# Decode attention with a mixer MLP on one core: x fetched as 16 rows, p turned half by half, exponents read from PSUM, maxima taken bank by bank

## The chip, the core and the metric

The kernel runs on one core of a Trainium2 chip. The metric is the device time of one launch in microseconds (us); the figure for a kernel is the median of its runs. The profile is one more execution, recorded by the hardware profiler.

## What is computed

For two batch rows `x` (2 x 1 x 1024, all in fp32) two branches are mixed by a gate:

```python
g = _sigmoid((x * gate_w).sum(-1, keepdims=True))
a = _A_ref(x, A_k_cache, A_v_cache, A_wq, A_wo)
b = _B_ref(x, B_w1, B_w2, B_w3, B_w4)
return g * a + (1 - g) * b
```

Branch A is attention for one new token against a long cache: 32 query heads share 4 key/value heads, the cache has 32768 positions of 128 numbers for each of the 8 pairs (batch row, key/value head). Branch B is a layer norm and a gelu MLP of 1024 -> 3584 -> 1024 (with one position the shifted part of the mixer adds nothing, so `w1` and `w2` are not used).

```python
q = (x @ wq) -> 32 heads of 128
scores = einsum("bhqd,bhkd->bhqk", q, k) * (Dh ** -0.5)
p = softmax(scores);  o = einsum("bhqk,bhkd->bhqd", p, v)
a = o @ wo
h2 = gelu(layernorm(x1) @ w3) @ w4          # x1 = x here;  b = x1 + h2
```

Every weight and the whole cache is read once: 331.37 MB.

## The kernel before, in words

**One stream through two buffers.** All large operands pass through two SBUF buffers, `buf_a` and `buf_b`, each 128 partitions of up to 64 KB. SyncE (SP) issues the loads in one fixed order (L554 to L567), alternating: `wq` to a, `w3` to b, `wq`, `w3`, then for every pair two loads of keys (`kt`, to a) and two of values (`vt`, to b), with `w4` and `wo` woven in. The first two loads go out at once. Every later one waits on the semaphore `go`, which VectorE (DVE) raises in `free()` (L284) when TensorE (PE) has finished with a buffer. So a buffer is loaded again only after its matmuls are over, and the DMA queue has work as long as one buffer is always issued before the other one's load ends. The last load (`w4`, second part) comes in five pieces (L571).

**Rounds.** PE runs 20 rounds (`rounds`, L136). In each it multiplies the load in `buf_a` (`sets(0, ...)`, into the two PSUM banks `ps_a`) and then that in `buf_b` (`sets(1, ...)`, into `ps_b`). The small stationary operands, `wt_a` and `wt_b`, hold x, the queries, or p; semaphores `ready[0]` and `ready[1]` say that they are filled. A pair takes two rounds: in the first its second scores meet the first half of its values, in the second the next pair's first scores meet the second half of its values.

**x.** ScalarE (ACT) fetches `xg` (x and the gate vector, laid out as 128 partitions of 24 numbers) with one DMA into `x2` (L195): each of the 64 rows of 48 numbers is read twice, once for the lower and once for the upper half of the partitions, and the access pattern has that factor of 2 outermost. DVE waits for it (`edge`, L319), shuffles it into `xs` (L322), and the gate, mean, variance and `wt_a` for the first `wq` load follow from it in a chain through DVE, PE and ACT (L326 to L359). No load's matmul can start before `wt_a` is there.

**From scores to p.** DVE takes the maximum over both banks (`scores`, L418) and copies the scores to SBUF (`keep`, L421); for a pair's second scores the maximum goes through a PE transpose, a reduction and a PE broadcast to become `bias` (L482 to L490). ACT then takes four exponents, one for each bank of the first and second scores (L217 to L220). Each is taken twice (`spread_rows`, L208), which writes p into all eight 128-column blocks of `p_dup` with every block twice. PE multiplies the eight blocks by the permutation `perm` (L161) into both banks of `tr`, and DVE copies `tr` into `wt_b` with two copies over 64 partitions (`turned`, L473). As each exponent fills all of `p_dup` and each turn all of `tr`, exponent, turn and copy of one bank are over before those of the next begin. A pair does this twice in its first round and twice in its second.

**Queries.** GpSimd (POOL) writes the next pair's queries to `wt_a` (L247) when `dp` says that the scores have been copied out of `ps_a`.

Of the kernel before, what the change touches and what calls it, by code (L numbers as in the profile page):

```python
# [24 lines left out]
E = 2  # L25
# [14 lines left out]
def kernel(  # L40
# [32 lines left out]
    ident, ones, perm = (sbuf(n, P) for n in ("ident", "ones", "perm"))  # L73
    r32 = sbuf("r32", C)
# [4 lines left out]
    mask_g, mask_r = sbuf("mask_g", 1), sbuf("mask_r", 1)  # L79
    x2 = sbuf("x2", 2 * KD * 3)  # L80
    xs = sbuf("xs", KD * 3)
# [8 lines left out]
    h_fin = sbuf("h_fin", FIN * C)  # L90
    mx, m1, bias = sbuf("mx", 2), sbuf("m1", 1), sbuf("bias", 1)
    m8, mb = sbuf("m8", REP, 1), sbuf("mb", P, 1)
# [11 lines left out]
    with tc.tile_critical(sync_engine=POOL, no_gpsimd_drain=True):  # L104
# [16 lines left out]

        def sets(x, which, event=False):
            last = None
# [6 lines left out]
            if event:  # L130
                last.then_inc(pd, 1)

# [3 lines left out]
        def rounds():  # L136
            with t.Fori(0, ROUNDS) as i:
                with t.If(i > 0):
                    sets(1, range(5, 8), True)
                    with odd(i):  # L140
                        take(t, dvp)
                        mm(sm[:, LP:LP + REP], ones, lsel).then_inc(pd, 1)
                        take(t, dvp)
                        for e in range(E):
                            last = mm(sm[:, OP + e * REP:OP + (e + 1) * REP],
                                      pv_t[:, e * P:(e + 1) * P], sel_all)
                        last.then_inc(pd, 1)
                take(t, landed[0], 16)
                take(t, ready[0])
                sets(0, range(8), True)  # L150
                with t.If(i < ROUNDS - 1):
                    with odd(i):
# [13 lines left out]
                take(t, piece, 16)  # L166
                sets(1, range(3, 5), True)
            done = 0
# [16 lines left out]
        with t.Fori(0, 2) as phase:  # L185
            with t.If(phase > 0):
                rounds()
            with t.Else():
                take(t, dvp)
# [5 lines left out]
        s.dma_start(x2, bass.AP(xg.tensor, xg.offset, [[0, 2], [2 * KD * 3, H], [1, 2 * KD * 3]])  # L195
                    ).then_inc(edge, 16)
        take(s, da)
# [5 lines left out]

        def spread_rows(src, bank, func, n, **kw):

            for d in range(2):
                more = kw if d == 0 else {k: x for k, x in kw.items() if k != "accum_out"}
                last = s.activation(at(p_dup, d * H, (512, 2), (P, 4), (1, H)),  # L208
                                    at(src, bank * 512, (1, 2), (P, 4), (2, H)), func, **more)
            last.then_inc(acp, n)  # L210

        for src in (qs, hs):
            take(s, da)
            spread_rows(src, 0, AF.Copy, 2)
# [9 lines left out]
        g_.memset(ident, 0.0)  # L224
        g_.drain()
        g_.affine_select(out=ident, in_=ident, compare_op=ALU.not_equal, fill=1.0, base=0,
                         pattern=[[-1, P]], channel_multiplier=1).then_inc(pc, 1)
        for tt in (sel, wt[0], wt[1], h_fin, buf[1][:, E * F * 2:], p_dup, lsel, pv_t):
            g_.memset(tt, 0.0)
# [70 lines left out]
        v.memset(mb, 0.0)  # L300
        v.wait_ge(pc, 1)
        v.tensor_reduce(r32, ident.rearrange("p (j c) -> p c j", j=G), axis=AX.X, op=ALU.add)
        for i in range(2):
            v.tensor_reduce(parity[:, i:i + 1], at(ident, i * C, (2 * C, 2), (1, C)), axis=AX.XY, op=ALU.add)
        for tau in range(2):
            for u in range(2):
                v.tensor_copy(at(perm, tau * H + u * C, (REP, G), (1, REP)),
                              at(ident, 16 * u + REP * tau, (C, G), (1, REP)))
        wait_order()
# [8 lines left out]

        v.wait_ge(edge, 16)  # L319
        for W in range(2):  # L320
            for tau, (lo, hi) in enumerate(halves):
                last = v.tensor_copy(at(xs, 12 * W, (6, E), (1, 6), rows=(lo, hi)),  # L322
                                     at(x2, 12 * W + 6 * tau, (24, E), (1, 6), rows=(lo, hi)))
        last.then_inc(dp, 1)
# [56 lines left out]

        got()
        free()
        first(qs, 0).then_inc(dp, 1)
        v.sem_inc(dvp, 2)
        got(4)
# [4 lines left out]
        x_to_hidden(1)  # L391
        v.sem_inc(dvp, 2)
        got(3)
        free()
        more(qs, 0).then_inc(da, 1)
        v.sem_inc(dvp, 3)
        got(3)
        for tau in range(2):
            last = v.tensor_reduce(at(qraw, REP * tau, (2 * REP, 8), (1, REP)),
                            at(tr, tau * H, (P, 8), (1, REP), (REP, G)), axis=AX.X, op=ALU.add)  # L400
        last.then_inc(dvp, 1)
        wait_order()
# [4 lines left out]
        last.then_inc(dp, 1)  # L407
        got(3)

# [3 lines left out]
        v.tensor_scalar_mul(acc_sb, hs, mask_r)  # L413
        got()
        free()

        def scores(L):
            v.reduce_max(out=mx[:, L:L + 1], in_=ps[0], axis=AX.X)  # L418

        def keep(L):  # L420
            v.tensor_copy(s_sb[:, L * 1024:(L + 1) * 1024], ps[0]).then_inc(dp, 1)  # L421

        scores(0)
        keep(0)
        v.sem_inc(dvp, 1)
        got()
        for u in range(2):
            for tau in range(2):
                if u and tau:
                    continue  # L430
                last = v.tensor_reduce(at(hid, 16 * u + REP * tau, (24, 8), (1, REP)),
                                at(tr, tau * H + u * C, (P, 8), (1, REP), (REP, G)), axis=AX.X, op=ALU.add)
        last.then_inc(dvp, 1)
        wait_order()
# [29 lines left out]
        got(3)  # L464
        free()
        masked(ps[1])
        wait_order()
        v.sem_inc(dvp, 2)
        got(2)

        def turned(b, to):
            for tau, (lo, hi) in enumerate(halves):
                last = v.tensor_copy(at(wt[1], b * H, (P, 8), (1, H), rows=(lo, hi)),  # L473
                              at(tr, tau * H, (P, 8), (1, H), rows=(lo, hi)))
            last.then_inc(to, 1)

        with v.Fori(0, PAIRS) as m:
            got()
            free()
            scores(1)  # L480
            wait_order()
            v.tensor_tensor(m1, mx[:, :1], mx[:, 1:], op=ALU.max).then_inc(dvp, 1)  # L482
            keep(1)
            got()
# [4 lines left out]
            got()  # L489
            v.tensor_copy(bias, sm[:, BP:BP + 1]).then_inc(da, 1)  # L490
            v.sem_inc(dvp, 1)
            got()
            v.sem_inc(da, 1)
            turned(0, dvp)
            got()
            v.sem_inc(da, 1)
            turned(1, ready[1])
            v.sem_inc(piece, 16)
            got(2)
            free()  # L500
            first(pvs, 1)
            got()
            free()
            scores(0)
            keep(0)
            v.sem_inc(dvp, 1)
            got()
            v.sem_inc(da, 1)
            turned(0, dvp)
            got()  # L510
            turned(1, ready[1])
            v.sem_inc(piece, 16)
# [27 lines left out]
        wait_order()  # L540
        got()
        masked(ps[0])
# [66 lines left out]
```

## Time and profile before

| | us |
|---|---|
| runs: median (lowest to highest) of 3 | 794.53 (793.89 to 796.43) |
| profiled execution, its own time | 796.01 |
| its span, first to last instruction | 794.2 |
| PE busy in the span | 472.9 (60%) |
| DVE busy | 159.5 (20%) |
| ACT busy | 54.5 (7%) |
| DMA queue of SP, share of 16 engines | 96.9% |

The page cuts the span into 40 slices of 19.9 us and gives the busy share of each engine in tenths. A wait is shown as idle time of an instruction, with what released it behind an arrow. In answers by window the columns are: window, its length, busy time and number of instructions on PE, PE's weight loads, DVE, ACT and POOL, then the granted PE clock, the DMA share and GB/s. A packet there is one row of a load (64 KB for a full buffer) or one completion mark.

### The profile page before, as it was taken

What the parts mean: (1) busy time and instruction counts of PE and PEld (TensorE: products, weight loads), DVE (VectorE), ACT (ScalarE), POOL (GpSimd) and SP (SyncE); (2) the same over time, 40 slices, a digit from 0 to 9 for tenths busy, and PEclk for the clock granted to TensorE, in tenths of its full rate; (3) what the DMA queues carried; (4) which work ended last, traced back from release to release, by engine and by line L of the source; (5) the groups of instructions that cost most, each with busy time, mean ns of one, the idle gap of its engine ahead of it and who ended that gap; (6) DMA issues with size and microseconds to landing.
All of it is one profiled execution on the core that took longest, in us unless ns stands there. A gap on an engine that the chain in (4) does not pass through costs nothing. (4 is left out here: it accounts for less than half of the span.)

```text
span 794.2 us, 8176 instructions
## 1 busy us (share of the span) xinstructions
PE 472.9 (60%) x3275; PEld 213.5 (27%) x3275; DVE 159.5 (20%) x326; ACT 54.5 (7%) x106; POOL 22.2 (3%) x93
## 2 busy tenths in 40 slices
PE   0064837558655774666566657655765576565757
PEld 0031313132313231422142314311432233133312
DVE  3020103020212122213112211221122122111221
ACT  0010000020002000200020002000100010001000
POOL 3000100000000000000000000000000000000000
PEclk9997969778866877788779767876787679678879
DMA  9919999999999999999999999999999999999997
GB/s 404 390 56 456 439 406 439 449 446 422 422 426 442 403 436 452 426 429 422 449 439 429 426 426 455 386 452 426 429 422 436 442 436 429 429 429 422 432 429 301
DMA packets 6486, 331.43 MB, mean 417 GB/s; under 512 B 842, under 2 KB 850, under 8 KB 1106
## 3 DMA queue, kind: packets, MB, share of 16 engines
q1 hardware_dynamic: 6352, 331.36, 96.9%
q10 hardware_dynamic: 130, 0.02, 0.0%
q14 instruction: 3, 0.02, 0.0%
q8 instruction: 1, 0.02, 0.0%
HBM read 331.37 MB, written 0.01 MB: 417 GB/s over the span
## 5 line engine op out<-in xcount | busy, mean ns | idle before, releaser
L119 PE MATMUL ps_a<-buf_a,wt_a 128*32 128x512 f32 x1280 | 184.7, 742 | 105.2 <-PEq L116 105.2
L119 PE MATMUL ps_b<-buf_b,wt_b 128*32 128x512 f32 x1256 | 163.2, 678 | 45.8 <-PEq L116 45.7
L119 PE MATMUL tr<-perm,p_dup 128*128 128x128 f32 x608 | 103.9, 342 | 60.3 <-PEq L116 60.3
L119 PEld LDWEIGHTS tr<-perm,p_dup 128*128 128x128 f32 x608 | 96.4, 249 | 72.9 <-issue 72.9
L119 PEld LDWEIGHTS ps_a<-buf_a,wt_a 128*32 128x32 f32 x1280 | 52.6, 132 | 228.4 <-issue 228.4
L119 PEld LDWEIGHTS ps_b<-buf_b,wt_b 128*32 128x32 f32 x1256 | 47.9, 123 | 148.3 <-issue 148.1
L208 ACT ACTIVATE p_dup<-s_sb,bias 128x512 f32<-128x512 f32 x64 | 47.5, 744 | 570.6 <-ACTq L116 570.6
L418 DVE TENSOR_REDUCE mx<-ps_a 128x1 f32<-128x1024 f32 x17 | 20.8, 1225 | 234.0 <-DVEq L116 234.0
L473 DVE COPY wt_b<-tr 64x512 f32<-64x512 f32 x64 | 44.1, 689 | 104.5 <-DVEq L116 103.1
L365 DVE TENSOR_TENSOR pvs<-pvs,ps_b 128x512 f32<-128x512 f32 x16 | 11.0, 688 | 87.6 <-DVEq L116 87.0
L119 PE MATMUL sm<-part,ones 128*128 128x4 f32 (+1 forms) x4 | 1.1, 350 | 43.8 <-PEq L116 43.8
L247 POOL COPY wt_a<-q_all 64x64 f32 (+1 forms) x64 | 12.3, 235 | 525.8 <-POOLq L116 525.4
L119 PE MATMUL sm<-sel_all,pv_t 128*128 128x8 f32 x40 | 7.9, 307 | 30.5 <-PEq L116 30.5
L421 DVE COPY s_sb<-ps_a 128x1024 f32<-128x1024 f32 x17 | 20.7, 1217 | 0.0
L369 DVE COPY pvs<-ps_b 128x512 f32<-128x512 f32 x8 | 5.5, 692 | 66.1 <-DVEq L116 66.1
L119 PEld LDWEIGHTS sm<-sel_all,pv_t 128*128 128x128 f32 x40 | 7.3, 256 | 31.0 <-issue 31.0
L119 PEld LDWEIGHTS sm<-part,ones 128*128 128x128 f32 x4 | 1.0, 313 | 43.9 <-issue 43.9
L154 PE MATMUL sm<-ident,m 128*1 128x128 f32 x9 | 2.4, 269 | 16.2 <-PEq L116 16.2
L119 PE MATMUL sm<-ones,mb 1*128 1x1 f32 x18 | 4.2, 299 | 11.2 <-PEq L116 11.2
L154 PEld LDWEIGHTS sm<-ident,m 128*1 128x1 f32 x9 | 0.7, 79 | 24.1 <-issue 24.1
L119 PEld LDWEIGHTS sm<-ones,mb 1*128 1x128 f32 x18 | 3.6, 250 | 12.9 <-issue 12.7
L322 DVE COPY xs<-x 64x12 f32<-64x12 f32 x4 | 0.7, 167 | 30.7 <-DMA x<-xg 30.7
(95 smaller groups left out, 95.9 us busy)
## 6 DMA issues: line engine op xcount, KB each, us to landing
buf_b<-w SPq DMA_DIRECT2D x3, 7168.0 KB, 28.6
buf_b<-w SPq DMA_DIRECT2D x1, 3072.0 KB, 17.4
buf_b<-w SPq DMA_DIRECT2D x1, 2048.0 KB, 21.9
buf_b<-w SPq DMA_DIRECT2D x1, 1024.0 KB, 23.9
buf_b<-w SPq DMA_DIRECT2D x2, 512.0 KB, 25.1
buf_a<-kt SPq DMA_DIRECT2D x16, 28.9
buf_b<-vt SPq DMA_DIRECT2D x16, 26.3
buf_a<-wq SPq DMA_DIRECT2D x2, 22.7
```

What stands on the lines that cost most here:

```text
L119: return t.matmul(o, lhsT, rhs, start=start, stop=stop, skip_group_check=True)
L154: t.transpose(sm[:1, MT:MT + P], m1, ident).then_inc(pd, 1)
L208: last = s.activation(at(p_dup, d * H, (512, 2), (P, 4), (1, H)), at(src, bank * 512, (1, 2), (P, 4), (2, H)), func, **more)
L247: last = g_.tensor_copy(at(wt[0], e * 512 + u * P + u * 16 + tau * REP, (256, 2), (C, G), (1, REP), rows=(lo, hi)), q_all[lo:hi, bass.ds(m ...
L322: last = v.tensor_copy(at(xs, 12 * W, (6, E), (1, 6), rows=(lo, hi)), at(x2, 12 * W + 6 * tau, (24, E), (1, 6), rows=(lo, hi)))
L365: last = v.tensor_add(dst, dst, ps[x][:, i * 512:i * 512 + 512])
L369: v.tensor_copy(dst, ps[x][:, :512])
L418: v.reduce_max(out=mx[:, L:L + 1], in_=ps[0], axis=AX.X)
L421: v.tensor_copy(s_sb[:, L * 1024:(L + 1) * 1024], ps[0]).then_inc(dp, 1)
L473: last = v.tensor_copy(at(wt[1], b * H, (P, 8), (1, H), rows=(lo, hi)), at(tr, tau * H, (P, 8), (1, H), rows=(lo, hi)))
```

## The change

Five things are changed; loads, their order, the matmuls on them and the end of the kernel are not.

1. **x as 16 rows.** `xg` is fetched into `x16`, 16 partitions of 192 numbers. PE spreads it to 128 partitions with eight matmuls against the 0/1 matrix `spread` into `tr`; DVE copies `xs` from there. `spread` needs one POOL memset and one DVE copy; the four DVE copies that built `perm` are gone.
2. **One exponent a bank.** ACT writes p once, 512 columns in a half of `p`, so two banks' p can stand side by side. The two exponents of the second scores read PSUM (`ps_a`) itself; only the first scores are still copied to SBUF. POOL's permission to write the next pair's queries comes from ACT after the four exponents, no longer from DVE after the copy of the second scores.
3. **Four transposes a half.** Each half of p is turned by four plain transposes into its own bank of `tr`, in place of eight multiplications by `perm` over both banks. PE no longer waits for DVE between the halves.
4. **The rearrangement moves to DVE.** `turned` makes four copies over 64 partitions of 256 numbers a half, in place of two of 512.
5. **Maximum by bank.** PE marks the end of each `ps_a` bank, and DVE takes the maximum of the first while PE fills the second. The buffer is freed before the second maximum.

The diff, cut to what is spoken of here:

```diff
-    p_dup = sbuf("p_dup", 1024)
-    s_sb = sbuf("s_sb", 2048)
+    p = sbuf("p", 1024)
+    s_sb = sbuf("s_sb", 1024)
...
-                sets(0, range(8), True)
+                sets(0, range(8), 5, 7)
...
-                    with t.Fori(0, 2):
+                    for q in range(2):
                         take(t, acp)
-                        take(t, dvp)
-                        for k in range(8):
-                            last = mm(tr[:, k * P:(k + 1) * P], p_dup[:, k * P:(k + 1) * P], perm)
+                        for j in range(4 * q, 4 * q + 4):
+                            last = t.transpose(tr[:, j * P:(j + 1) * P], p[:, j * P:(j + 1) * P], ident)
                         last.then_inc(pd, 1)
...
             with t.Else():
+                take(t, edge, 16)
+                take(t, dvp)
+                for e in range(E):
+                    for w in range(4):
+                        last = mm(tr[:, e * 24:e * 24 + 24], spread[:, w * P:(w + 1) * P],
+                                  x16[:, (2 * w + e) * 24:(2 * w + e + 1) * 24], w == 0, w == 3)
+                last.then_inc(pd, 1)
...
-        s.dma_start(x2, bass.AP(xg.tensor, xg.offset, [[0, 2], [2 * KD * 3, H], [1, 2 * KD * 3]])
-                    ).then_inc(edge, 16)
+        s.dma_start(x16, xg.rearrange("(j q) k c -> j (q k c)", j=16)).then_inc(edge, 16)
...
-        def spread_rows(src, bank, func, n, **kw):
-
-            for d in range(2):
-                more = kw if d == 0 else {k: x for k, x in kw.items() if k != "accum_out"}
-                last = s.activation(at(p_dup, d * H, (512, 2), (P, 4), (1, H)),
-                                    at(src, bank * 512, (1, 2), (P, 4), (2, H)), func, **more)
-            last.then_inc(acp, n)
+        def turn(src, bank, func, to, *dims, **kw):
+
+            return s.activation(at(p, to, *dims, (1, H)), at(src, bank * 512, (1, 2), (P, 4), (2, H)), func, **kw)
...
             for i in range(NI):
                 take(s, da)
-                spread_rows(s_sb, i, AF.Exp, 1, bias=bias, scale=scale, accum_out=l4[:, i:i + 1])
+                turn((s_sb, ps[0])[i // 2], i % 2, AF.Exp, i % 2 * 512, (256, 2), (H, 4), bias=bias, scale=scale,
+                     accum_out=l4[:, i:i + 1]).then_inc(acp, 1)
+            s.drain().then_inc(dp, 1)
...
         def scores(L):
-            v.reduce_max(out=mx[:, L:L + 1], in_=ps[0], axis=AX.X)
+            for i in range(2):
+                got()
+                if i:
+                    free()
+                v.reduce_max(out=mx[:, 2 * L + i:2 * L + i + 1], in_=ps[0][:, i * 512:(i + 1) * 512], axis=AX.X)
...
-        def turned(b, to):
-            for tau, (lo, hi) in enumerate(halves):
-                last = v.tensor_copy(at(wt[1], b * H, (P, 8), (1, H), rows=(lo, hi)),
-                              at(tr, tau * H, (P, 8), (1, H), rows=(lo, hi)))
-            last.then_inc(to, 1)
+        def turned(q, first_to, to):
+            got()
+            for kp, src in enumerate(halves):
+                for tau, dst in enumerate(halves):
+                    last = v.tensor_copy(at(wt[1], kp * P + q * H, (2 * P, 4), (REP, G), (C, 2), (1, REP), rows=dst),
+                                         at(tr, q * 512 + tau * REP, (P, 4), (C, G), (16, 2), (1, REP), rows=src))
+                    if kp == tau == 0 and first_to:
+                        last.then_inc(first_to, 1)
+            if to:
+                last.then_inc(to, 1)
```

Where it moves instructions, shown at two places. First ACT, from the start of the program (before): the fetch of x, the small functions of the gate, and in the last rows the eight exponents of a pair, two for each bank.

```order
2 L195 DMA x<-xg 128x1x48
3 L198 ACT_TABLE_LOAD [waits dve_to_act]
...
14 L208 ACTIVATE p_dup,l<-s_sb,bias 128x8x64 [waits dve_to_act]
15 L208 ACTIVATE p_dup<-s_sb,bias 128x8x64
16 L208 ACTIVATE p_dup,l<-s_sb,bias 128x8x64 [waits dve_to_act]
17 L208 ACTIVATE p_dup<-s_sb,bias 128x8x64
```

The same engine now; the exponents of the second scores read `ps_a`.

```order
2 L201 DMA x<-xg 16x192
3 L203 ACT_TABLE_LOAD [waits dve_to_act]
...
14 L211 ACTIVATE p,l<-s_sb,bias 128x512 [waits dve_to_act] x2
15 L211 ACTIVATE p,l<-ps_a,bias 128x512 [waits dve_to_act] x2
```

The fetch keeps its place at the head of ACT and has 16 rows in place of 128; a pair has four exponents in place of eight.

Then DVE in the first round of a pair, before: maximum of the second scores (`mx`, `m`), their copy to `s_sb`, the bias, the copies of turned p to `wt_b`, and the first sums of the values (`pvs`).

```order
61 L418 TENSOR_REDUCE mx<-ps_a 128x1 [waits pe_to_dve]
62 L482 TENSOR_TENSOR m<-mx 128x1
63 L421 COPY s_sb<-ps_a 128x1024
64 L485 TENSOR_REDUCE m<-sm 1x8 [waits pe_to_dve]
65 L487 TENSOR_SCALAR mb<-m 1x128
66 L490 COPY bias<-sm 128x1 [waits pe_to_dve]
```

The same stretch now, up to the sums.

```order
59 L420 TENSOR_REDUCE mx<-ps_a 128x1 [waits pe_to_dve] x2
60 L480 TENSOR_REDUCE m<-mx 128x1
61 L482 TENSOR_REDUCE m<-sm 1x8 [waits pe_to_dve]
62 L484 TENSOR_SCALAR mb<-m 1x128
63 L487 COPY bias<-sm 128x1 [waits pe_to_dve]
64 L470 COPY wt_b<-tr 64x4x4x2x8 [waits pe_to_dve]
65 L470 COPY wt_b<-tr 64x4x4x2x8 x3
66 L470 COPY wt_b<-tr 64x4x4x2x8 [waits pe_to_dve]
67 L470 COPY wt_b<-tr 64x4x4x2x8 x3
```

The copy of the second scores has left the stretch between the maximum and the bias, the maximum is two instructions, and each half of p is brought to `wt_b` by four copies.

More of the change, by code (lines that the diff above doesn't have):

```diff
@@ L69 @@
     wt = [sbuf("wt_a", C * C), sbuf("wt_b", C * C)]
-    p_dup = sbuf("p_dup", 1024)
-    s_sb = sbuf("s_sb", 2048)
+    p = sbuf("p", 1024)
+    s_sb = sbuf("s_sb", 1024)
     qs, hs, acc_sb, pvs = (sbuf(n, 512) for n in ("qs", "hs", "acc_sb", "pvs"))
-    ident, ones, perm = (sbuf(n, P) for n in ("ident", "ones", "perm"))
+    ident, ones = (sbuf(n, P) for n in ("ident", "ones"))
+    spread = sbuf("spread", 4 * (P + 1), 16)
     r32 = sbuf("r32", C)
@@ L119, in mm, with sets @@
             return t.matmul(o, lhsT, rhs, start=start, stop=stop, skip_group_check=True)
[L122 to L123 removed]
+        def sets(x, which, *events):
             for n4 in which:
@@ L301 @@
         v.wait_ge(pc, 1)
+        v.tensor_copy(at(spread, 0, (P + 1, 4), (H, 2), (4, 16), rows=(0, 16)),
+                      at(ident, 0, (0, 4), (0, 2), (1, 16), rows=(0, 16))).then_inc(dvp, 1)
         v.tensor_reduce(r32, ident.rearrange("p (j c) -> p c j", j=G), axis=AX.X, op=ALU.add)
@@ L489 @@
             got()
[L490 to L497, printed above, removed]
+            v.tensor_copy(bias, sm[:, BP:BP + 1]).then_inc(da, 2)
+            turned(0, da, None)
+            turned(1, da, ready[1])
             v.sem_inc(piece, 16)
@@ L501 @@
             first(pvs, 1)
-            got()
-            free()
             scores(0)
[L505 to L511, printed above, removed]
+            keep()
+            turned(0, None, None)
+            turned(1, None, ready[1])
             v.sem_inc(piece, 16)
```

75 lines of the change are left out of this document (29 added, 46 removed).

## The prediction

> **What bounds the kernel now.** I read the page first, for the shares of DMA by slice.
>
> ```profile
> DMA  9919999999999999999999999999999999999997
> GB/s 404 390 56 456 439 406 439 449 446 422 422 426 442 403 436 452 426 429 422 449 439 429 426 426 455 386 452 426 429 422 436 442 436 429 429 429 422 432 429 301
> ```
>
> The 16 DMA engines are full in every slice but the third and the last; no other engine is busy over 60% of the span. So the stream of loads is the bound, and a change can pay only where the stream stands still. Busy time by window, cut at the places where the rate changes, says how much that is (the last two numbers are DMA share and GB/s):
>
> ```profile
> 0.00:39.00 39.00, 0.00 (x0) 0.00 (x0) 6.09 (x16) 0.00 (x0) 7.53 (x22) 1.00 0.95 404
> 39.00:56.40 17.40, 10.62 (x68) 3.56 (x68) 3.60 (x21) 2.94 (x4) 0.24 (x1) 1.00 0.01 1
> 56.40:78.00 21.60, 11.62 (x102) 6.37 (x102) 2.23 (x6) 0.00 (x0) 0.24 (x1) 0.84 1.02 431
> 78.00:187.00 109.00, 68.85 (x492) 29.47 (x492) 19.26 (x45) 8.53 (x15) 4.09 (x17) 0.80 1.00 434
> 187.00:771.00 584.00, 365.20 (x2469) 169.04 (x2469) 124.91 (x235) 43.08 (x87) 10.12 (x52) 0.77 1.00 431
> ```
>
> The undisturbed rate is 434 GB/s. Between 39.00 and 56.40 nothing flows: 17.4 us. From 187 to 771 the rate is 431, 3 GB/s short, worth 584 x 3/434 = 4.0 us (2.7 to 5.4, as both rates are rounded). The window up to 39 is short too: its 404 GB/s x 39 us = 15.76 MB would take 36.3 us at 434, which leaves 2.7 us, some 1.8 of them before the first packet.
>
> Why the hole? The timeline of the start:
>
> ```profile
> 0.89 0.39 SPq L567 DMA_DIRECT2D buf_a<-wq  x1
> 0.89 1.10 ACTq L195 DMA_DIRECT2D x<-xg  x1
> 40.20 0.71 DVE L322 COPY xs<-x 64x12 f32<-64x12 f32 x4 [30.67 <-DMA x<-xg]
> 41.64 0.56 PE L119 MATMUL sm<-part,ones 128*128 128x4 f32 x2 [41.64 <-PEq L116]
> 45.84 9.50 PE L119 MATMUL ps_a<-buf_a,wt_a 128*32 128x512 f32 x64 [0.88 <-PEq L116]
> 55.55 0.33 SPq L567 DMA_DIRECT2D buf_a<-wq  x1
> ```
>
> x, 24 KB, is issued at 0.89 with the first load and reaches DVE at 40.20, after both first loads have gone through. Only then comes the chain to `wt_a` (5.64 us), the first matmuls (9.71 us to the next issue), and the third load. Both buffers sat full and unread.
>
> Why so late? The DMA views of 7.5 to 7.8 us, of 10 to 20, and of 39 to 56.4 give these packets (q10 carries x, q1 the loads):
>
> ```profile
> q10 hardware_dynamic: 2, 0.00, 0.6%
> ```
> ```profile
> q1 hardware_dynamic: 72, 4.72, 108.9%
> q10 hardware_dynamic: 10, 0.00, 0.1%
> ```
> ```profile
> q10 hardware_dynamic: 100, 0.02, 0.5%
> ```
>
> The page counts the queue's whole traffic, and the view of 791 to 794.2 us that of the output, whose eight rows are the only thing left then:
>
> ```profile
> q10 hardware_dynamic: 130, 0.02, 0.0%
> ```
> ```profile
> DMA packets 16, 0.01 MB, mean 3 GB/s; under 512 B 8, under 2 KB 16, under 8 KB 16
> ```
>
> x's 130 packets are 128 rows and two more; the output's 16 are eight rows of 1 KB and eight small ones. I read the small ones as one completion mark for each engine that takes part: x then runs on two engines and the output on eight, and both fit the outermost count of the access pattern (2 and 8). While the loads flow, 72 load rows pass in 10 us, 4.5 an engine, and 10 rows of x, 5 on each of two engines: one row of x between two rows of a load. A load row of 64 KB (8 MB over 128 rows) at 434/16 GB/s takes 2.42 us. With 64 rows an engine and one every 2.42 us, x cannot end before the loads: 100 of its 130 packets go in the hole.
>
> **The fetch of x.** It now has 16 rows, so by that reading 16 engines take one row each plus a completion mark. The first packets of x came in the 7.5 to 7.8 view, 7.65 say; the mark follows one turn later, 7.65 + 2.42 = 10.1. Bounds: 7.7 if row and mark go in one turn, 12.5 with one turn more. Before DVE can use x, PE spreads it: eight matmuls of two passes each, by the row of 41.64 (0.56 for two passes) 16 x 0.28 = 4.5, plus about 0.25 for the handoff. The rest of the chain stays at 5.64. So `wt_a` is ready at 10.1 + 4.75 + 5.64 = 20.5 (18.1 to 22.9). What `spread` needs before that, a POOL memset and a DVE copy, lies in the first 10 us. The four copies of `perm` that go with it took 4.5 us in all beside POOL's memsets, by their group (busy time and mean ns after the first bar); a copy of `spread` as slow as that, begun near 2 us, is over by 7.
>
> ```profile
> L307 DVE COPY perm<-ident 128x32 f32<-128x32 f32 x4 | 4.5, 4314 | 0.0
> ```
>
>
> What is late next is the load itself, by the DMA views of 0 to 39 and of 39 to 56.4 us (last number: us from issue to landing):
>
> ```profile
> buf_a<-wq SPq DMA_DIRECT2D x1, 23.0
> ```
> ```profile
> buf_a<-wq SPq DMA_DIRECT2D x1, 22.4
> ```
>
> The first `wq` load lands at 0.89 + 23.0 = 23.9, 3.4 us after `wt_a`. Matmuls then start at 23.9 and the third load is issued at 23.9 + 9.71 = 33.6. An issue takes under 1 us to its first packet (55.55 to the window's edge at 56.40), so the third load is queued at 34.6, and the first two keep the engines busy until 38 or later. The hole closes, with 3.4 us to spare; x may come 3.4 + 3.4 = 6.8 us later than 10.1 before any of it reopens. Nor does it open one load later: the second buffer lands by 40, its matmuls take at most the same 9.7, and its next issue near 50 meets a third load that flows until 38 + 19.4 = 57. **Term: -17.4 us**, and perhaps the 0.9 left over in the first window, which I do not count.
>
> **From scores to p.** In the steady state I look for late issues, in the DMA view of a single issue each, at 264.61, 496.85, 653.73 (values, issued in a pair's first round), 198.48 and 451.45 (keys; values of a second round):
>
> ```profile
> buf_b<-vt SPq DMA_DIRECT2D x1, 22.6
> ```
> ```profile
> buf_b<-vt SPq DMA_DIRECT2D x1, 24.5
> ```
> ```profile
> buf_b<-vt SPq DMA_DIRECT2D x1, 22.4
> ```
> ```profile
> buf_a<-kt SPq DMA_DIRECT2D x1, 30.5
> ```
> ```profile
> buf_b<-vt SPq DMA_DIRECT2D x1, 29.4
> ```
>
> The load issued at 55.55 into an idle queue landed after 22.4 us. Two first-round loads of values took 22.4 and 22.6, so they too found the queue run dry, and a third had 2.1 us in hand; the others shown have 7 to 8. So the chain ahead of the first-round values is the only one that runs late, and I put the 4.0 us down to it. One such round:
>
> ```profile
> 393.80 1.23 DVE L418 TENSOR_REDUCE mx<-ps_a 128x1 f32<-128x1024 f32 x1 [15.06 <-DVEq L116]
> 396.63 1.57 POOL L247 COPY wt_a<-q_all 64x64 f32 x8 [76.38 <-POOLq L116]
> 397.87 0.75 ACT L208 ACTIVATE p_dup<-s_sb,bias 128x512 f32<-128x512 f32 x1 [38.19 <-ACTq L116]
> 399.65 3.76 PE L119 MATMUL tr<-perm,p_dup 128*128 128x128 f32 x16 [2.21 <-PEq L116]
> 403.64 1.39 DVE L473 COPY wt_b<-tr 64x512 f32<-64x512 f32 x2 [5.90 <-DVEq L116]
> 403.68 0.75 ACT L208 ACTIVATE p_dup<-s_sb,bias 128x512 f32<-128x512 f32 x1 [4.33 <-ACTq L116]
> 411.00 7.07 PE L119 MATMUL ps_b<-buf_b,wt_b 128*32 128x512 f32 x64 [1.78 <-PEq L116]
> 418.27 0.33 SPq L567 DMA_DIRECT2D buf_b<-vt  x1
> 423.00 8.66 PE L119 MATMUL ps_a<-buf_a,wt_a 128*32 128x512 f32 x64 [4.93 <-PEq L116]
> ```
>
> The group of the two exponents of a bank, and of the read that follows the first:
>
> ```profile
> L208 ACT ACTIVATE p_dup<-s_sb,bias 128x512 f32<-128x512 f32 x64 | 47.5, 744 | 570.6 <-ACTq L116 570.6
> L208 ACT ACTIVATION_READ_ACCUMULATOR p_dup<-s_sb,bias 128x1 f32 x32 | 6.0, 188 | 0.0
> ```
>
> Exponent, turn and copy of one bank take 403.68 - 397.87 = 5.81 us, and two follow each other. Now the maximum after the last matmul is half as long (-0.6) and the copy of the scores is out of DVE's way (about -0.5). One exponent with its read takes 0.74 + 0.19 = 0.93 where two took 1.7; four transposes take half of 3.76, 1.9; four copies of 256 numbers lie between 4 x 0.35 (half of one of 512, itself 1.39/2) and 4 x 0.70, and I take 1.8, nearer to the half plus a start. Exponent and transposes of the second bank run beside the copies of the first. So p is ready near 396.9 + 0.9 + 2 x 1.9 + 1.8 + 0.5 = 403.9, 7 us before 411.00 (at 0.70 a copy, 6 us). The issue moves from 418.27 to about 411 and no longer finds an empty queue. More lead is worth nothing: the stream takes it up. **Term: -2.5 us** of the 4.0, since not all of that shortage need be this; bounds 0 and -4.0. The second round gains a few us in the same way, which buys nothing, with 7 us in hand already.
>
> New waits: POOL's queries wait for ACT's four exponents. The last of those starts when PE has turned the second half, near 402, so the queries end near 405, against 423.00, where `ps_a` is next written.
>
> **The sum.** 17.4 + 2.5 = 19.9. Against the profiled execution: span 794.2 - 19.9 = 774.3, own time 796.01 - 19.9 = 776.1. The median of the runs lies 1.5 below that execution, so I predict 794.53 - 19.9 = **774.6 us**.
>
> **Rivals.**
>
> *x on two engines still.* Engines may go by partitions, eight each; 16 rows would lie on two. The Trainium skill, "DMA: Bandwidth & Descriptors", states "Partitions per engine | 8 (convention)" in its Specifications, while its section "Why a DMA increments its semaphore by 16 and not by 1" derives the number of engines from the outermost counts of the two access patterns, which gives 2 before and 16 now. Against the first rule stands the trace: x's old target covered all 128 partitions and still brought two marks. Price: eight turns and a mark, 7.65 + 8 x 2.42 = 27.0; `wt_a` at 37.4, third load issued at 47.1 and not at 55.55, 8.4 gained, and 2.5 as above: 783.6. Chance 0.04.
>
> *x behind both loads.* If all rows share one engine, 17 turns of 2.42 from 7.65 end near 48, so in fact when the loads have gone, as now, and PE's spreading (4.75) is added to the path, 0.9 less at best: 794.53 + 3.9 - 2.5 = 795.9. For it: nothing in the trace; 128 rows of a load use all engines. Chance 0.03, within the noise.
>
> *Slower: `ps_a` held by ACT.* The second scores stay in PSUM until four exponents are done, where a copy in the first three us had saved them. The next pair's matmuls then wait for four steps s and POOL: 397.87 + 4s + 1.57. At s = 5.81, as now, that is 422.7, just before 423.00. The load of keys has some 7 us of lead (30.5 - 22.4 is 8.1), so it costs time from s = 7.5, and eats the whole gain where each of eight pairs is 2.5 us beyond that, from s = 8.2. At s = 9 the delay is 12.4 - 7 = 5.4 us a pair, 43 in all: 774.6 + 43 = 818. Against it: no part of the new step is longer than 2.8 us, and its parts overlap. Chance 0.03.
>
> **How the numbers follow.** The forecast has 0.90. Its own low end takes every term in full, 17.4 + 0.9 + 4.0 = 22.3, and the lowest run (0.64 under the median): 771.6. Its high end takes the hole alone, 777.1, and the highest run (1.9 above): 779.0. The rivals have 0.10, which may be left out, so the range is **771.6 to 779.0**. A measurement of this kernel tells about 0.3%, 2.4 us, from no change. Faster by more than that: the forecast and the two-engine rival, 0.94. Same: 0.03. Slower: 0.03.
>
> **What would show it right or wrong.** Right: q10 has 32 packets; the copy of `xs` starts near 15 us; the third load is issued between 32 and 36; DMA is full in the third slice; first-round loads of values land 26 us or more after issue; p is ready 10 us after the maximum starts, where it took 17. Wrong: a stretch over 2 us without traffic before 700, an `xs` copy after 22, a wait of PE for `wt_a` in the pairs' loop while `buf_a` is full, or a rate from 187 on that stays at 431 with all loads well in hand (then the 4.0 us has another cause).

## The result, and the profile after

| | before | changed |
|---|---|---|
| median of 6 runs | 796.78 us | 775.81 us |
| lowest to highest | 793.89 to 798.91 | 775.43 to 776.12 |
| profiled execution, own time / span | 796.01 / 794.2 | 776.02 / 774.2 |

The ratio is 0.9739, with a 95% interval of 0.9717 to 0.9762: 21 us less. Against the profiled execution of before the difference is 20.0 us, where 19.9 was forecast; the span came out at 774.2, where 774.3 was forecast. That these two agree to 0.1 us is luck, as single runs of before differ by 5 us. The median of 774.6 was 1.2 low through two errors that partly cancel: the three runs behind it are the lowest three of the six of before, 2.25 us under the median of all, and the gain is 21.0 and not 19.9.

The page of the changed kernel, DMA share and GB/s by slice, and the queue that carries x:

```profile
DMA  9999999999999999999999999999999999999996
GB/s 377 434 433 434 427 440 433 433 434 433 430 433 433 433 437 433 433 433 433 433 433 433 433 433 433 433 433 433 433 433 433 433 433 433 433 437 433 433 425 279
...
q10 hardware_dynamic: 32, 0.01, 0.0%
```

The third slice is full, and the rate hardly wanders from slice to slice: it is 433 in most of them. q10 has 32 packets: 16 rows and 16 completion marks. By window, the place of the hole and the steady state (columns as before):

```profile
39.00:56.40 17.40, 10.67 (x70) 3.38 (x70) 1.57 (x5) 0.00 (x0) 0.00 (x0) 0.75 1.10 478
78.00:187.00 109.00, 60.94 (x417) 19.62 (x417) 22.23 (x50) 6.00 (x12) 2.04 (x11) 0.76 1.00 433
187.00:750.00 563.00, 303.90 (x2037) 100.32 (x2037) 122.10 (x293) 22.03 (x56) 10.12 (x52) 0.72 1.00 433
```

Where 1 GB/s flowed now 478 do (a window this short is uneven). From 187 us on the rate is 433, where it was 431. Such a rate is coarse: the 16 rows that the engines move at a time are 1.05 MB, so a window's edge before or after them shifts the rate of 563 us by up to 1.9 GB/s. The row times further on are the firmer measure. The timeline of the start:

```profile
0.90 0.41 ACTq L201 DMA_DIRECT2D x<-xg  x1
2.32 5.04 DVE L308 COPY spread<-ident 16x128 f32<-16x128 f32 x1 [0.98 <-POOL ident L232]
10.64 3.57 PE L120 MATMUL tr<-x,spread 16*128 16x24 f32 x16 [10.64 <-PEq L117]
14.37 0.71 DVE L326 COPY xs<-tr 64x12 f32<-64x12 f32 x4 [4.38 <-DVEq L117]
18.57 0.56 PE L120 MATMUL sm<-part,ones 128*128 128x2 f32 x2 [2.19 <-PEq L117]
25.00 9.85 PE L120 MATMUL ps_a<-buf_a,wt_a 128*32 128x512 f32 x64 [5.87 <-PEq L117]
35.05 0.33 SPq L553 DMA_DIRECT2D buf_a<-wq  x1
```

x is there by 10.6, `xs` is copied at 14.37 where it was 40.20, and PE then waits 5.87 us, now for the load itself, which lands at 24.7. The third load goes out at 35.05, 20.5 us sooner, while the second still flows. The first round of a pair that stands beside the one shown of before:

```profile
374.56 0.69 DVE L420 TENSOR_REDUCE mx<-ps_a 128x1 f32<-128x512 f32 x1 [12.85 <-DVEq L117]
376.37 0.69 DVE L420 TENSOR_REDUCE mx<-ps_a 128x1 f32<-128x512 f32 x1 [1.12 <-DVEq L117]
379.35 0.75 ACT L211 ACTIVATE p<-s_sb,bias 128x512 f32<-128x512 f32 x1 [72.45 <-ACTq L117]
380.34 1.94 PE L160 MATMUL tr<-ident,p 128*128 128x128 f32 x8 [1.42 <-PEq L117]
381.57 3.50 DVE L470 COPY wt_b<-tr 64x256 f32<-64x256 f32 x8 [2.35 <-DVEq L117]
382.11 0.69 ACT L211 ACTIVATE p<-ps_a,bias 128x512 f32<-128x512 f32 x1 [1.17 <-ACTq L117]
384.93 1.57 POOL L253 COPY wt_a<-q_all 64x64 f32 x8 [76.17 <-POOLq L117]
385.52 8.79 PE L120 MATMUL ps_b<-buf_b,wt_b 128*32 128x512 f32 x64 [3.25 <-PEq L117]
394.52 0.33 SPq L553 DMA_DIRECT2D buf_b<-vt  x1
404.88 9.35 PE L120 MATMUL ps_a<-buf_a,wt_a 128*32 128x512 f32 x64 [10.56 <-PEq L117]
```

The maximum that follows the keys' last matmul is now the second one. From there to the matmuls on the values it takes 385.52 - 376.37 = 9.2 us, where it took 411.00 - 393.80 = 17.2; over the eight first rounds 9.1 to 10.4, where it took 16.2 to 17.4. POOL's queries end at 386.5, 18 us before `ps_a` is written again (404.88), so the scores that stay in PSUM hold nobody up. The load of values goes out 28.6 to 29.8 us after the keys' landing, where it was 33.5 to 35.7. That is less than the chain gained, because the 64 matmuls on the values take 8.7 to 9.9 us now and took 7.1 to 8.7; the mean granted clock is 0.749 here and was 0.798. The section on DMA issues, for the loads of values:

```profile
buf_b<-vt SPq DMA_DIRECT2D x16, 28.8
```

28.8 us from issue to landing (median), where it was 26.3: the issue is early enough in both rounds.

### The profile page after: what moved, and what is told of

Read it like the earlier page. It is cut to its first block, busy times and chain, and to the rows that moved or that the text cites. A ratio compares the mean times of both kernels' runs of the same rounds, so it can differ in the third digit from the quotient of the medians.

```text
span 774.2 us, 7184 instructions
## 1 busy us (share of the span) xinstructions
PE 418.0 (54%) x2835; PEld 140.1 (18%) x2835; DVE 162.3 (21%) x393; ACT 32.2 (4%) x74; POOL 22.6 (3%) x94
## 5 line engine op out<-in xcount | busy, mean ns | idle before, releaser
L120 PE MATMUL ps_b<-buf_b,wt_b 128*32 128x512 f32 x1256 | 181.3, 741 | 120.1 <-PEq L117 120.1
L420 DVE TENSOR_REDUCE mx<-ps_a 128x1 f32<-128x512 f32 x34 | 23.5, 692 | 266.5 <-DVEq L117 266.5
L470 DVE COPY wt_b<-tr 64x256 f32<-64x256 f32 x128 | 53.9, 421 | 18.7 <-DVEq L117 16.9
L211 ACT ACTIVATE p<-s_sb,bias 128x512 f32<-128x512 f32 x16 | 12.0, 750 | 539.1 <-ACTq L117 539.1
L160 PE MATMUL tr<-ident,p 128*128 128x128 f32 x152 | 26.2, 322 | 14.5 <-PEq L117 14.1
L369 DVE TENSOR_TENSOR pvs<-pvs,ps_b 128x512 f32<-128x512 f32 x16 | 11.0, 688 | 109.3 <-DVEq L117 108.7
L253 POOL COPY wt_a<-q_all 64x64 f32 (+1 forms) x64 | 12.2, 234 | 529.7 <-POOLq L117 529.2
L160 PEld LDWEIGHTS tr<-ident,p 128*128 128x128 f32 x152 | 19.8, 163 | 24.4 <-issue 24.3
L211 ACT ACTIVATE p<-ps_a,bias 128x512 f32<-128x512 f32 x16 | 11.0, 687 | 15.4 <-ACTq L117 15.4
L423 DVE COPY s_sb<-ps_a 128x1024 f32<-128x1024 f32 x9 | 10.9, 1214 | 0.0
L120 PE MATMUL tr<-x,spread 16*128 16x24 f32 x16 | 3.6, 382 | 10.6 <-PEq L117 10.6
L512 DVE SCALAR_TENSOR_TENSOR tmp<-pvs,mss,tmp 128x128 f32<-128x128 f32 x16 | 5.6, 351 | 1.2
L375 DVE TENSOR_TENSOR pvs<-pvs,ps_b 128x512 f32<-128x512 f32 x8 | 5.5, 688 | 0.6
L379 DVE SCALAR_TENSOR_TENSOR acc_sb<-ps_b,mask_g,acc_sb 128x512 f32<-128x512 f32 x4 | 3.0, 751 | 12.4 <-DVEq L117 12.2
## 6 DMA issues: line engine op xcount, KB each, us to landing
buf_b<-w SPq DMA_DIRECT2D x2, 512.0 KB, 25.1
buf_a<-kt SPq DMA_DIRECT2D x16, 28.8
buf_b<-vt SPq DMA_DIRECT2D x16, 28.8
buf_a<-wq SPq DMA_DIRECT2D x2, 24.9
```

The costliest lines, as they stand in the source:

```text
L120: return t.matmul(o, lhsT, rhs, start=start, stop=stop, skip_group_check=True)
L160: last = t.transpose(tr[:, j * P:(j + 1) * P], p[:, j * P:(j + 1) * P], ident)
L211: return s.activation(at(p, to, *dims, (1, H)), at(src, bank * 512, (1, 2), (P, 4), (2, H)), func, **kw)
L253: last = g_.tensor_copy(at(wt[0], e * 512 + u * P + u * 16 + tau * REP, (256, 2), (C, G), (1, REP), rows=(lo, hi)), q_all[lo:hi, bass.ds(m ...
L369: last = v.tensor_add(dst, dst, ps[x][:, i * 512:i * 512 + 512])
L375: return v.tensor_add(dst, dst, ps[x][:, 512:])
```

## The experiments

**Theory A**: the hole is x on two engines, one row of x between two rows of a load; the shortage of 4 us later on comes from late issues in the first round of a pair, which the shorter way to p ends; everything else is covered by the stream. The **rivals** (B to G) stand in the expectations. Experiments 1 to 4 ran on one chip, 5, 6 and 8 on another, 7 and 9 on a third, each beside runs of before, whose medians there were 797.6 to 798.4 us. The changed kernel ran beside the six runs of before in the result's table alone, so a time "above the changed kernel" compares two sets of runs.

**1. The new fetch of x alone**, on the kernel before.

```diff
-        s.dma_start(x2, bass.AP(xg.tensor, xg.offset, [[0, 2], [2 * KD * 3, H], [1, 2 * KD * 3]])
-                    ).then_inc(edge, 16)
+        s.dma_start(x16, xg.rearrange("(j q) k c -> j (q k c)", j=16)).then_inc(edge, 16)
...
+                        last = mm(tr[:, e * 24:e * 24 + 24], spread[:, w * P:(w + 1) * P],
+                                  x16[:, (2 * w + e) * 24:(2 * w + e + 1) * 24], w == 0, w == 3)
...
```

> Before with the new fetch of x alone (16 rows, spread by PE). Theory A (the hole is x's two engines, the shortage from 187 us on is the late first-round values, which the new turning of p ends): the hole closes and nothing else, so about 18 us under before on the same chip, 2.5 to 3 us above the changed kernel; loads of first-round values still land 22 to 25 us after issue, and the rate from 187 us on stays at 431 GB/s. Rival B (the shortage has another cause, such as the late start itself): the same time as the changed kernel, 20 to 21 us under before, and 433 GB/s.

Measured: 779.72 us (777.24 to 783.49), ratio 0.9776 (0.9743 to 0.9809), so by the ratio 17.9 us under before (15.3 to 20.5; the medians lie 18.7 apart). The hole is closed, and the shortage stays. Busy time by window, and the DMA view of the issue at 559.33, a first-round load of values:

```profile
187.00:750.00 563.00, 349.92 (x2385) 163.91 (x2383) 117.86 (x222) 41.59 (x84) 9.64 (x50) 0.78 1.00 429
```
```profile
buf_b<-vt SPq DMA_DIRECT2D x1, 22.8
```

The eight first-round loads land 22.8 to 25.0 us after issue; before, it was 22.4 to 24.6. Rival B falls: the shortage is not a matter of the late start.

**2. The new way to p alone**: the changed kernel with the old fetch of x.

```diff
-        s.dma_start(x16, xg.rearrange("(j q) k c -> j (q k c)", j=16)).then_inc(edge, 16)
+        s.dma_start(x2, bass.AP(xg.tensor, xg.offset, [[0, 2], [2 * KD * 3, H], [1, 2 * KD * 3]])
+                    ).then_inc(edge, 16)
...
```

> The changed kernel with the old fetch of x (128 rows from a pattern with 2 outermost). Theory A: the hole from 39 to 56 us stays, 2.5 to 3 us under before; first-round values land 28 us or more after issue and the rate after the hole is 433 GB/s throughout. Rival B: the same as before within 1 us. If the p change carries more than I think: over 5 us under before.

Measured: 793.51 us (792.85 to 794.35), ratio 0.9945 (0.9926 to 0.9963): 4.4 us under before by the ratio (3.0 to 5.9; the medians lie 4.9 apart). The windows show both halves of theory A:

```profile
39.00:56.40 17.40, 11.66 (x75) 4.50 (x76) 3.32 (x20) 2.94 (x4) 0.24 (x1) 1.00 0.01 1
187.00:750.00 563.00, 304.00 (x2039) 100.62 (x2039) 121.90 (x286) 22.03 (x56) 9.65 (x50) 0.73 1.00 434
```

The hole is there whole, and the rate after it is the undisturbed 434. First-round values land after 28.2 to 29.9 us. The two parts give 17.9 and 4.4, together 22.3 against 21.0 for the whole change; the intervals cover the difference.

**3. x's 16 rows on two engines.** The rows are read in another order, so that the outermost count of the source is 2; they land in the same 16 partitions, and `spread` puts them right.

```diff
-        s.dma_start(x16, xg.rearrange("(j q) k c -> j (q k c)", j=16)).then_inc(edge, 16)
+        s.dma_start(x16, bass.AP(xg.tensor, xg.offset, [[192, 2], [2 * 192, 8], [1, 192]])).then_inc(edge, 16)
...
```

> The changed kernel with x's 16 rows read in the order 0, 2, ... 14, 1, 3, ... 15, so that the outermost count of the source is 2; the rows land in the same 16 partitions. Theory A (the outermost count sets the engines, and each engine takes one row of x between two rows of a load): q10 has 18 packets, x takes 8 turns and a mark, 5.0 + 8 x 2.42 = 24.4; copy of xs near 28.3, third load issued near 44, a hole of some 5.5 us from 39 on: about 781.5 us. Rival C (engines go by target partitions, or a transfer this small goes through at once): 32 packets or a copy of xs near 14, and the changed kernel's time.

Measured: 781.51 us (781.41 to 782.62). The DMA view of the start, and the timeline:

```profile
q10 hardware_dynamic: 18, 0.01, 0.1%
```
```profile
0.90 1.22 ACTq L201 DMA_DIRECT2D x<-xg  x1
28.82 0.71 DVE L326 COPY xs<-tr 64x12 f32<-64x12 f32 x4 [18.84 <-DVEq L117]
44.14 0.33 SPq L553 DMA_DIRECT2D buf_a<-wq  x1
```

18 packets are 16 rows and two marks. `xs` is copied at 28.82 (28.3 expected), the third load goes out at 44.14 (44), the time is 781.51 (781.5). In part that is luck: the trace's packet records (start and length of each row and mark) have the first row of x at 7.4 us and not at 5.0, and the last two rows of each engine in one turn, so seven turns were needed from a start one turn later; the marks begin at 24.3 and 24.4. The turns themselves, 2.4 us each, are as counted. The partitions are those of the changed kernel, so it is the outermost count and not the partitions that sets the engines; rival C falls, and with it the prediction's rival of eight partitions an engine.

**4. The old fetch, ahead of the loads.** The kernel before, with its 128 rows of x issued by SP as the first thing on the loads' own queue.

```diff
-        s.dma_start(x2, bass.AP(xg.tensor, xg.offset, [[0, 2], [2 * KD * 3, H], [1, 2 * KD * 3]])
-                    ).then_inc(edge, 16)
...
+        sy.dma_start(x2, bass.AP(xg.tensor, xg.offset, [[0, 2], [2 * KD * 3, H], [1, 2 * KD * 3]])
+                     ).then_inc(edge, 16)
         for j, (x, src) in enumerate(loads):
```

> Before with one thing changed: the same 128-row fetch of x is issued by SP ahead of the first load, not by ACT beside it. Theory A (x was late because its rows took turns with the loads' rows): on the same queue its 64 rows an engine go first, in about 1 us, x is there by 5 us, the hole closes, and the time is that of the new fetch alone, about 18 us under before, with 1 us lost at most on two engines. Rival D (128 small rows on two engines are slow by themselves): x comes after 15 us and part of the hole stays.

Measured: 780.19 us (777.44 to 781.64), ratio 0.9770 (0.9741 to 0.9800). The timeline:

```profile
0.89 0.70 SPq L562 DMA_DIRECT2D x<-xg  x1
1.65 0.42 SPq L567 DMA_DIRECT2D buf_a<-wq  x1
9.44 0.70 DVE L320 COPY xs<-x 64x12 f32<-64x12 f32 x4
```

The same 128 rows, again with two marks (q1 has 130 packets more than before), begin between 2.3 and 3.3 us by the packet records, and are there before DVE gets to them at 9.44. What made x late was taking turns with the loads, not its rows; rival D falls.

**5. p later by one set of copies.** In the changed kernel DVE makes the copies to `wt_b` twice.

```diff
         def turned(q, first_to, to):
             got()
+            for kp, src in enumerate(halves):
+                for tau, dst in enumerate(halves):
+                    v.tensor_copy(at(wt[1], kp * P + q * H, (2 * P, 4), (REP, G), (C, 2), (1, REP), rows=dst),
+                                  at(tr, q * 512 + tau * REP, (P, 4), (C, G), (16, 2), (1, REP), rows=src))
+            wait_order()
...
```

> The changed kernel with DVE's copies of the turned p into the second weight tile made twice, so that p is ready 3.5 us later in each round. Theory A (the stream bounds; lead beyond what keeps the queue filled is worth nothing): no change, 775 to 776.5 us, but first-round values land some 3.5 us sooner after issue, 25 to 26 and not 28 to 29.5 us. Rival E (the chain from scores to p lies on the path in each pair): 8 x 3.5 = 28 us more, about 804.

Measured: 775.84 us (775.57 to 776.12), the changed kernel's time. One first round in its timeline:

```profile
374.62 0.69 DVE L420 TENSOR_REDUCE mx<-ps_a 128x1 f32<-128x512 f32 x1 [1.12 <-DVEq L117]
386.75 9.97 PE L120 MATMUL ps_b<-buf_b,wt_b 128*32 128x512 f32 x64 [6.32 <-PEq L117]
396.92 0.33 SPq L558 DMA_DIRECT2D buf_b<-vt  x1
```

The second maximum, at 374.62 here, was at 376.37 in the changed kernel; from there to the matmuls it takes 12.1 us and not 9.2 (mean of the eight first rounds 12.2 and not 9.7). First-round values land after 26.5 to 28.0 us, with 1 to 2 us more lead left than I expected, and nothing is lost. Rival E falls: 2.5 us more on the way to p, or 3.0 in the round shown, cost nothing.

**6 and 7. p later by three sets, and by two.** The same loop run three times more (6) and twice more (7).

```diff
         def turned(q, first_to, to):
             got()
+            for again in range(3):
...
```

> The changed kernel with DVE's copies of the turned p made four times, so that p is ready 10.3 us later in the first round of a pair. Theory A: the lead of 6.6 us there is used up, the stream stops for 3.7 to 4.2 us in each of eight first rounds, first-round values land after 22.4 us, second rounds just hold: 800 to 815 us. Rival E: 8 x 10.3 = 82 us more, about 858. If late issues do not cost the stream anything: as the changed kernel.

Measured: 790.11 us (786.56 to 792.96), 14.3 above the changed kernel. First-round values land after 21.8 to 22.6 us, so all eight find the queue empty or nearly so. In these windows no row begins (the last columns again share and GB/s; a packet counts where it starts, so rows begun before may still run):

```profile
169.50:172.80 3.30, 3.07 (x33) 0.77 (x25) 0.77 (x2) 0.00 (x0) 0.00 (x0) 1.00 0.00 0
250.90:253.30 2.40, 1.83 (x24) 0.40 (x16) 0.74 (x2) 0.00 (x0) 0.00 (x0) 1.00 0.00 0
331.50:333.40 1.90, 1.37 (x16) 0.32 (x12) 0.76 (x2) 0.00 (x0) 0.00 (x0) 1.00 0.00 0
411.50:411.90 0.40, 0.00 (x0) 0.00 (x0) 0.33 (x2) 0.00 (x0) 0.00 (x0) 1.00 0.02 0
490.00:490.40 0.40, 0.00 (x0) 0.00 (x0) 0.33 (x2) 0.00 (x0) 0.00 (x0) 1.00 0.02 0
568.40:568.90 0.50, 0.00 (x0) 0.00 (x0) 0.43 (x2) 0.00 (x0) 0.00 (x0) 1.00 0.01 0
```

The other two rounds have such windows too, 646.9 to 647.4 and 725.3 to 725.9. The direction is theory A's, the size is not: the windows begin near the 3.7 us that I gave to each of eight and shrink to 0.4. I took this for a sign that the true lead is 8.9 us, worked out from the loop of a pair (rival G), and tested that with two more sets:

> The changed kernel with DVE's copies of the turned p made three times, p ready some 6.7 us later in a first round. Theory G (the true lead follows from the loop of a pair: landing of the second-round values after 21.9, the keys' stream 19.4, their matmuls 9, the chain to p 9.2, the matmuls on the values 9, in all 68.5 of the 77.4 us that four loads take, so 8.9 us are free): no change, 775.5 to 776.5. Theory A as I first sized it (lead 6.6, from landing times): the stream just stops, 0.1 us and the slow first rows of a restart, 0.6 us, in each of eight rounds: 779 to 782.

Measured: 781.58 us (778.83 to 783.91), 5.8 above the changed kernel, inside theory A's numbers and clear of G's. First-round values land after 22.7 to 24.9 us, the picture of the kernel before, and the rate is that of before too:

```profile
187.00:750.00 563.00, 293.29 (x2033) 100.31 (x2033) 219.02 (x520) 22.03 (x56) 9.71 (x50) 0.74 1.00 430
```

From the second maximum to the matmuls on the values it takes, in one first round of each:

```profile
377.79 0.69 DVE L420 TENSOR_REDUCE mx<-ps_a 128x1 f32<-128x512 f32 x1 [1.12 <-DVEq L117]
393.87 6.61 PE L120 MATMUL ps_b<-buf_b,wt_b 128*32 128x512 f32 x44 [10.16 <-PEq L117]
```
```profile
383.21 0.69 DVE L420 TENSOR_REDUCE mx<-ps_a 128x1 f32<-128x512 f32 x1 [1.12 <-DVEq L117]
402.43 8.38 PE L120 MATMUL ps_b<-buf_b,wt_b 128*32 128x512 f32 x64 [13.52 <-PEq L117]
```

16.1 us with two sets more (the first pair of rows) and 19.2 with three, against 9.2: delays of 6.9 and 10.1 in the rounds shown, 6.2 and 9.6 in the mean of eight. So this delay in the changed kernel brings back the shortage and its price, with everything else new. G falls.

Where the time goes can be read from the packets. In the five us from 497, right after a first-round issue of before, and from 472.6 in the changed kernel:

```profile
q1 hardware_dynamic: 45, 1.90, 106.7%
```
```profile
q1 hardware_dynamic: 33, 2.16, 99.9%
```

1.90 MB are 29 rows (the other 16 packets are marks). They took 106.7% of 16 x 5 us, so 2.94 us each; the changed kernel's 33 rows took 2.42. The table adds up, from the packet records, what the engines lose around the eight first-round issues, by standing idle and by rows that take longer than 2.42 us:

| kernel | keys' landing to issue of first-round values, us | lost at the eight issues, us |
|---|---|---|
| before | 33.5 to 35.7 | 3.5 |
| changed | 28.6 to 29.8 | 0.1 |
| p later by one set (5) | 30.1 to 31.6 | 0.1 |
| p later by two sets (7) | 33.4 to 35.6 | 4.1 |
| p later by three sets (6) | 37.2 to 39.0 | 15.7 |

So nearly all of the 4.0 us of before lies at these issues. At the keys' landing two loads stand ahead of the values in the queue, 38.7 us of stream. In experiment 6 the first three issues come 38.6 to 39.0 us after the landing and lose 4.0, 3.1 and 2.8 us; the last five come after 37.2 to 37.4 and lose 1.2 each. Most of this difference of 1.4 us is PE's: its matmuls on keys and values take 17.2 to 17.4 us together in the last five, 18.0 to 18.6 in the first three. So the third set of copies brought the loss from about half a us an issue to three or four us in three rounds and to 1.2 in the other five, not to three in all eight. G had the dry queue about right, 8.9 us away where 38.7 - 29.1 = 9.6 are measured; what it lacked is that an issue some four us short of that already costs.

**8. The old fetch ahead, with the new way to p**: experiment 2 with the fetch of experiment 4.

> The changed kernel without its fetch of x: the old 128-row fetch, issued by SP ahead of the first load, and no spreading by PE. Theory A (all that counts in x is that it does not take turns with the loads): as the changed kernel within 1 us, perhaps 0.8 us more because the first load is issued 0.8 us later. Rival F (16 rows on 16 engines are needed for the whole gain): 2 us or more above the changed kernel.

Measured: 776.42 us (776.18 to 776.77), ratio 0.9733 (0.9696 to 0.9771), 0.6 us above the changed kernel, and that without the 16 rows, `spread` and its matmuls. Rival F falls. The 0.6 us would fit the first load's issue, 0.75 us later than in the changed kernel (1.64 against 0.89), but two sets of runs are compared here.

**9. The last load in four pieces**, as the stream is now full up to its end.

```diff
-PIECES = (6, 4, 2, 1, 1)
+PIECES = (6, 4, 2, 2)
```

> The changed kernel with the last load cut into pieces of 6, 4, 2, 2 of its 14 columns and not 6, 4, 2, 1, 1. With the stream full from 1.9 us on, what is left to gain lies at its end. The two last pieces of 0.5 MB leave the stream at 196 GB/s in the window 766 to 770; one piece of 1 MB should flow at 408, about 1.2 us sooner, and PE has eight more matmul passes after the last landing, 0.64 us: 775.2, 0.5 us under the changed kernel. If the slow end comes from something else than the size of the pieces: 776.4.

Measured: 776.06 us (775.94 to 776.32): no gain shows, though 0.5 us is near what two sets of runs can tell. The timelines of the last matmuls, of the changed kernel and of this one:

```profile
770.22 0.64 PE L120 MATMUL acc<-buf_b,h_fin 128*32 128x256 f32 x8 [0.16 <-PEq L117]
771.02 0.42 DVE L533 COPY o_sb<-acc 128x256 f32<-128x256 f32 x1 [2.08 <-DVEq L117]
```
```profile
769.82 1.07 PE L120 MATMUL acc<-buf_b,h_fin 128*32 128x256 f32 x16 [0.43 <-PEq L117]
771.06 0.42 DVE L533 COPY o_sb<-acc 128x256 f32<-128x256 f32 x1 [2.46 <-DVEq L117]
```

The last matmuls start 0.40 us sooner and last 0.43 longer: what the larger piece gives it takes back.

## Why the prediction was right, step by step

- **The bound.** Right. The stream of loads sets the time. DVE's copies doubled cost nothing (5); stops of the stream cost about what they last: in the first 60 us of experiment 3 the engines stood idle 6.1 us more than in the changed kernel, and it took 5.7 longer.
- **x's arrival.** Forecast 10.1, PE starts at 10.64. The turns and the marks are shown by experiment 3; that the number fits so well is partly luck. The issue is shorter, 0.41 us against 1.10, and by the packet records x's rows begin at 5.0 to 5.6 us, one turn sooner than the 7.65 assumed. Their marks begin at 7.6 to 9.3, a turn later as forecast, and PE starts 1.4 us after the last of them, a step that the sum did not have.
- **The chain to the first matmuls.** Forecast ready at 20.5; the last matmul of the chain starts at 18.57, so the chain is over near 20. The DVE copy of `spread` took 5.04 us beside POOL's memsets, as slow as allowed for, and hidden. The wait is for the load, as forecast; its matmuls started at 25.00 and not 23.9, the third load at 35.05 and not 33.6, both within the spare time. One reading was wrong, though the 5.64 us stand: they are not the way to `wt_a`. In the timeline of before POOL has filled `wt_a` by 41.31, and what the first matmuls at 45.84 follow is PE's own order, the second of the two sums for gate and layer norm:

```profile
41.07 0.24 POOL L240 COPY wt_a<-xs 128x64 f32<-128x64 f32 x1 [31.98 <-POOLq L116]
44.39 0.56 PE L119 MATMUL sm<-part,ones 128*128 128x2 f32 x2 [2.19 <-PEq L116]
```

- **The hole, -17.4.** Right: 17.9 with the new fetch alone (15.3 to 20.5), and 793.51 - 775.81 = 17.7 between the kernels with and without it.
- **The way to p, -2.5.** The mechanism was right and the size was off: this term measured 4.4 (3.0 to 5.9), and experiment 1 lies 3.9 above the changed kernel. I had taken 2.5 of the 4.0 that the rate showed, in case not all of it was this; nearly all of it was, 3.5 us at the eight issues by the table above. With 17.4 + 4.0 from the median of all six runs of before, 796.78, the sum is 775.4, against 775.81. The bounds of 2.7 to 5.4 were too narrow for their source, as the edges of a window of 109 us alone shift its rate by up to 9.6 GB/s; the 434 holds by the rows' 2.42 us. Which of the changes on this way (exponents, transposes, copies, maxima) brings how much was not tried apart.
- **Parts of that way.** A copy takes 3.50/8 = 0.44 us in the round shown, so 1.75 for four (1.8 forecast). From the maximum after the last matmul to the matmuls on the values 9.1 to 10.4 us, forecast 10.1.
- **The new wait of POOL for ACT.** Free, as forecast: over at 386.5, needed at 404.88.
- **The rivals' prices.** Two engines: experiment 3. The slower rival's price was not reached; experiments 6 and 7 measured a related one, that of p coming late, and showed that multiplying the excess over the lead by eight rounds overstates it. Two of its figures are a little off: with 7 us of lead it costs time from s = 7.6 and eats the gain from 8.3; and 17 turns from 7.65 end at 48.8. No price hangs on that.

## What to carry to other kernels

Where one stream of loads is the bound, look for the slices in which it stands still, and then for what the issue of the next load waits for; here a fetch of 24 KB held the third load back by 20 us. A small transfer that took turns with large rows cost, on its busiest engine, about one large row's time for each of its rows and one for the mark. So spread it over all engines by its outermost count, or issue it ahead of the loads on their own queue, which here was worth the same. The time from issue to landing tells the lead of a load: near 22 us the queue was empty, up to 25 us time was still lost, and from 26.5 us on more lead bought nothing.

## What the runs showed that was not expected

- **Lead steadies the time.** The kernels whose first-round values land 25.1 us or less after issue vary by 4 to 10 us from run to run: before by 5.0 to 10.3 in four sets of runs, experiment 1 by 6.2, 4 by 4.2, 6 by 6.4, 7 by 5.1. Those with 26.5 us or more vary by 0.4 to 1.5: the changed kernel by 0.7, experiment 2 by 1.5, 3 by 1.2, 5 by 0.6, 8 by 0.6, 9 by 0.4. That the lead is the reason is argued from this order alone; experiments 5 to 7, which differ in nothing but DVE's copies, agree with it.
- **The edge is soft.** A load that is issued some four us before the queue runs dry already costs: of the eight issues of before, those up to 34.3 us after the keys' landing lose under 0.1 us each, those from 34.6 on 0.2 to 1.3. The loss is mostly rows that take longer than 2.42 us right after the issue, 2.5 of the 3.5 us. Why they do was not found.
- **ACT's issue was longer over two engines.** 16 rows over two engines took ACT 1.22 us to issue, over 16 engines 0.41, and 128 rows over two engines 1.10. SP took 0.70 for those same 128 rows.
